# Splitting the last gather of a recurrent step into two column halves, with separate PSUM tiles for the turned halves and new issue orders

## The chip, the cores and the metric

The kernel runs on one core of a Trainium2 chip. A core has a matrix engine (TensorE, "PE" in the profile, with its weight loads as "PEld"), a vector engine (DVE), a scalar engine (ACT), a general engine (POOL) and a queue engine that issues transfers (SP; POOL issues some too). [...] The engines run their own instruction streams in order and wait for each other through semaphores.

The metric is the device time of one execution in microseconds, as the median of several runs. Before the change it is 3058.38 us (3 runs, 3051.87 to 3061.96).

## The reference

The computation is the forward and backward pass of a sum of two branches over a layer-normed input xn of 2048 rows and 512 columns: a dense branch (squared ReLU), and an attention branch that runs over 64 segments of 32 rows and hands 8 memory rows from one segment to the next. The attention branch, forward:

```python
for s in range(n_seg):                       # 64 segments of 32 rows
    h = concat([mem, x[segment s]])          # 8 memory rows + 32 rows
    q, k, v = h @ Wq, h @ Wk, h @ Wv         # 32 heads of 128
    p = softmax(mask(q k^T * scale))
    o = (p v) @ Wo                           # sum over the 32 heads
    mem = o[:8]                              # goes into the next segment
    outs.append(o[8:])
```

The result is `x + attention(xn) + dense(xn)`, and the kernel returns it with the gradients of the input, of the first memory, of the four attention weights and of the dense weights and biases for a given output gradient. Both directions of the attention are recurrent: forward, a segment's memory rows come out of the sum over heads of the segment before; backward, the gradient of a segment's memory rows comes out of three such sums (over Wq, Wk and Wv) of the segment after it.

## The kernel before

The kernel has five stages, one after the other: the dense branch with the layer norm; the forward chain of 64 steps; a stage that takes the backward pass of the memory rows ("left" rows) as far as it does not depend on the chain, with the dense weight gradients; the backward chain of 64 steps; and the attention's weight gradients. The change touches the two chains.

A step has 32 rows, so the kernel stacks four groups of eight heads into the 128 partitions. A matmul has weights of 32 columns and stands at one of four column positions of the array (`tile_position=(0, 32 * g)`), and four of them run beside each other. Work on heads is done in two halves of four heads per group, written 0 and 1 below.

In the **forward chain** (function `fwd`, lines 806 to 907) a step s computes, by the names used in the issue order: `k0mm q0mm k1mm q1mm v0mm v1mm` (projections, line 392), `..ev` (eviction from PSUM), `..fl` and `..Te` (a turn by matmul, line 165, and its eviction), `s0 s1` (scores, lines 432 and 437), `mx sb ex su rc pm` (softmax pieces on DVE and ACT), `tu` (turn of the probabilities, line 450), `w0 w1` (probabilities times values, line 547, into two pairs of PSUM banks with the tags pp0 and pp1), `oa ob` (their evictions), and `g0 g1` (the **gather**, line 460: the 32 heads times Wo, summed over the eight heads of each group into one PSUM bank R of 128 x 512). Then the end of the step: `ra rb` copy the two column halves of R into a float32 tile R4 in SBUF, one on ACT and one on DVE; `ta tb` turn R4 by four float32 matmuls with an identity (line 469) into one PSUM bank T; `HT` sums T over the four head groups for the 8 memory rows (line 482) and writes them into the next step's input X; `xt` does the same for the 24 other rows, later.

In the **backward chain** (function `bwd`, lines 1218 to 1356) a step has `o0mm o1mm` (projection of the gradient with turned Wo), `o0fl o0te` and so on, `vp0 vp1` (gradient of the values, lines 1290 and 1292), `s0 s1`, `d1 d2 d3 d4` for either half (the softmax's gradient on DVE, lines 496 to 506), `kp0 kp1 qp0 qp1` (line 547, into pp0 and pp1), evictions `kea keb qea qeb kla klb vea veb vla vlb`, six gathers `vg0 vg1 kg0 kg1 qg0 qg1` that add up in one bank R, and the same end `ra rb ta tb HT xt`. Its rows for kp and qp (`b_qN`, `b_kN`, `b_P`) come by transfers that POOL issues (`ldq ldn ldp`), others by SP (`ldk` for `b_kLs`, `vtr` for `b_vl`); POOL also makes two copies, `vc` and `pb` (lines 1252, 1253 and 1239).

Names with `L.` belong to the left rows, once in a block of four steps: in the forward chain `L.S0 L.S1 L.W0 L.W1 L.G0 L.G1 L.P0..P5 L.BT` on the matrix engine, in the backward chain `L.G0..3 L.H0..3 L.I0..3`, each eight matmuls, with `L.ra0..3` on DVE or ACT.

What runs in which order is written out by hand. `F_ORDER` and `B_ORDER` hold four lists of names, one for each step of a block; `play` (line 581) goes through them and calls each name's function, where each trailing `-` or `+` moves the name one step back or ahead (one block, with `L.`). All engines take their instructions in that order, each its own. `ENGS` says which evictions go to ACT and which to DVE. PSUM is allocated from pools as tiles: four single banks (tag "r", function `big`) that serve projections, turns, scores, R, T and left rows in turn, and the two pairs pp0 and pp1. A new tile in a bank waits until the last use of the tile before it, and instructions of two engines on one bank are kept apart.

Steps are called kind 0 to 3 below, by s mod 4 in order of issue.

## Time and profile before

| what | value |
|---|---|
| median of 3 runs | 3058.38 us (3051.87 to 3061.96) |
| profiled execution: span from first to last instruction | 3059.8 us, 109712 instructions |
| PE busy in the span | 2705.4 us (88%), 48600 matmuls |
| DVE / ACT / POOL busy | 1319.5 / 994.7 / 658.0 us |
| dense stage, up to about 297 us | 297 us, PE busy 259.4 |
| forward chain, 297 to 1179 us | 882 us, PE busy 813.4 |
| left rows backward, 1179 to 1470 us | 291 us, PE busy 216.3 |
| backward chain, 1470 to 2415 us | 945 us, PE busy 852.6 |
| weight gradients, 2415 to 3060 us | 645 us, PE busy 563.7 |
| mean granted clock of the matrix engine | 0.971 |

The profile shows one execution. A row of a timeline has its start and its length in microseconds, the engine, the source line, the operation, the tiles (output, then inputs after the arrow), the shape and a count; in brackets stands how long the engine had been idle and which engine's instruction released it. A row that merges several instructions runs from the first one's start to the last one's end. Matmuls are pipelined: one of 512 columns shows 0.38 us, but the next starts before it ends, so busy time of PE is more than the time that it streams.

### The profile page before, as it was taken

How to read it: one execution, taken by the hardware profiler on the slowest of the kernel's cores; microseconds unless marked ns; L12 is line 12 of the kernel's file. 1: busy time of each engine (PE TensorE's matmuls, PEld its weight loads, DVE VectorE, ACT ScalarE, POOL GpSimd, SP SyncE). 2: the span in 40 equal slices, each digit the busy share in tenths (PEclk: the TensorE clock that was granted, in tenths of full speed). 3: DMA queues.
4: the chain of work that ended last, by engine and by line, in shares of the span. 5: the costliest groups of instructions: out<-in, count | busy, mean ns of one | idle time of the engine just before them, and what ended most of it. 6: DMA issues, size and time to landing. Idle time of an engine off the chain costs nothing. (4 is left out here: it accounts for less than half of the span.)

```text
span 3059.8 us, 109712 instructions
## 1 busy us (share of the span) xinstructions
PE 2705.4 (88%) x48600; PEld 1386.8 (45%) x48600; DVE 1319.5 (43%) x3581; ACT 994.7 (33%) x2306; POOL 658.0 (22%) x1264
## 2 busy tenths in 40 slices
PE   8997899999999886877799899998989559999998
PEld 4453444444444444446444444444444224444443
DVE  5452566666666664334345444544545201100010
ACT  2422444444444444323333333333333101111111
POOL 0000000000000000113343433434343213322222
PEclk9998999999999998999999999999999879999999
DMA  9548375766767767777577676776777899898991
GB/s 257 185 146 250 101 188 161 189 181 172 190 168 182 165 157 192 229 230 220 149 173 174 190 187 164 177 203 169 176 200 175 238 192 217 194 211 207 204 207 39
DMA packets 794559, 566.78 MB, mean 185 GB/s; under 512 B 579409, under 2 KB 681570, under 8 KB 790754
## 3 DMA queue, kind: packets, MB, share of 16 engines
q1 hardware_dynamic: 748322, 430.47, 58.8%
q0 software_dynamic: 40528, 126.53, 13.5%
q8 instruction: 381, 6.24, 0.9%
q10 hardware_dynamic: 5232, 2.75, 0.4%
q14 instruction: 96, 0.79, 0.1%
HBM read 193.61 MB, written 238.56 MB: 141 GB/s over the span
## 5 line engine op out<-in xcount | busy, mean ns | idle before, releaser
L1505 PE MATMUL ps_gw<-gn,HNc 128*128 128x512 bf16 x1920 | 416.4, 379 | 0.0
L1505 PEld LDWEIGHTS <-HNc 128*128 128x128 bf16 x1920 | 187.8, 98 | 223.9
L374 ACT CAST f_N<-ps_proj 128x512 bf16<-128x512 f32 x320 | 185.9, 581 | 243.9 <-PE ps_proj L392 223.4
L1476 ACT CAST wt<-ps_gw 128x512 bf16<-128x512 f32 x128 | 74.4, 586 | 503.5 <-PE ps_gw L1505 474.4
L392 PEld LDWEIGHTS <-X 128*32 128x32 bf16 x6144 | 153.3, 97 | 161.3 <-DVE X L482 13.9
L835 POOL COPY kM<-f_kT 128x256 bf16<-128x256 bf16 x64 | 25.6, 401 | 786.7 <-DVE f_kT L377 594.9
L1459 DVE TENSOR_TENSOR gx<-ps_rows,gb 128x512 f32<-128x512 f32 x16 | 11.1, 692 | 420.5 <-PE ps_rows L1457 418.2
L1505 PE MATMUL ps_gw<-GOc,gn 128*128 128x512 bf16 x640 | 142.2, 385 | 54.8 <-DMA GOc<-S_GM 54.8
L460 PE MATMUL ps_gR<-Wk,gk 128*32 128x512 bf16 x2048 | 146.7, 386 | 19.4 <-ACT gk L374 12.9
L392 PE MATMUL ps_proj<-Wk,X 128*32 128x512 bf16 x2048 | 135.4, 384 | 12.6 <-DVE X L482 6.9
L460 PE MATMUL ps_gR<-Wq,gq 128*32 128x512 bf16 x2048 | 141.6, 382 | 1.2 <-issue 1.2
L374 ACT CAST gk<-b_pp 128x256 bf16<-128x256 f32 x192 | 68.8, 377 | 208.3 <-PE b_pp L547 146.6
L1477 POOL DMA_DIRECT2D out_dram<-wt x128 | 69.2, 541 | 309.5 <-ACT wt L1476 309.4
L1239 POOL COPY PD<-b_P 32x320 bf16<-32x320 bf16 x256 | 114.9, 449 | 95.3 <-PE b_pp L1292 64.4
L460 PE MATMUL ps_gR<-Wv,gv 128*32 128x512 bf16 x2048 | 133.4, 379 | 0.3 <-issue 0.3
L392 PE MATMUL ps_proj<-Wo,GT 128*32 128x512 bf16 x2048 | 123.9, 384 | 7.9 <-POOL GT L1203 6.7
L392 PE MATMUL ps_proj<-Wq,X 128*32 128x512 bf16 x2048 | 128.7, 382 | 0.0
L460 PE MATMUL ps_R<-Wo,OT 128*32 128x512 bf16 x2048 | 126.4, 388 | 0.0
L469 PE MATMUL ps_sum<-identF,R 128*128 128x128 f32 x512 | 102.4, 295 | 24.6 <-ACT R L374 18.4
L392 PE MATMUL ps_proj<-Wv,X 128*32 128x512 bf16 x2048 | 124.1, 378 | 0.0
L1505 PEld LDWEIGHTS <-gn 128*128 128x128 bf16 x640 | 63.4, 99 | 132.3 <-issue 59.6
L374 ACT CAST gON<-ps_proj 128x512 bf16<-128x512 f32 x128 | 74.9, 585 | 143.2 <-PE ps_proj L392 141.5
(260 smaller groups left out, 5128.0 us busy)
## 6 DMA issues: line engine op xcount, KB each, us to landing
S_A<-f_N SPq DMA_DIRECT2D x64, 512.0 KB
out_dram<-wt POOLq DMA_DIRECT2D x142, 128.0 KB, 4.6
S_A<-f_N SPq DMA_DIRECT2D x64, 256.0 KB
S_GB<-gv SPq DMA_DIRECT2D x32, 512.0 KB
S_GB<-gq SPq DMA_DIRECT2D x32, 512.0 KB
S_GB<-gk SPq DMA_DIRECT2D x32, 512.0 KB
b_kN<-S_A POOLq DMA_DIRECT2D x63, 256.0 KB, 5.0
b_qN<-S_A POOLq DMA_DIRECT2D x63, 256.0 KB, 5.4
```

Source lines behind the costliest of these rows:

```text
L374: nc.scalar.copy(out, in_)
L392: nc.tensor.matmul(o, lhsT=hT[:, dc, :], rhs=x, start=(dc == 0), stop=(dc == DC - 1), tile_position=(0, 32 * g))
L460: nc.tensor.matmul(o, lhsT=XT(k, g), rhs=x, start=(first and k == 4 * h), stop=(last and k == 4 * h + 3), tile_position=(0, 32 * g))
L469: nc.tensor.transpose(st["T"][:, c * P:(c + 1) * P], R4()[:, c * P:(c + 1) * P], identF[:])
L835: o["km"] = lambda: nc.gpsimd.tensor_copy(B_["kM"][:, :, :, lc], T["kT"][:, :, :, 0:M])
L1239: nc.gpsimd.tensor_copy(PD[32 * g:32 * g + 32, g], C["P"][32 * g:32 * g + 32, :, 0:L])
L1459: nc.vector.tensor_tensor(out=gx[:], in0=ps[:], in1=gb[:], op=ALU.add)
L1476: nc.scalar.copy(wt[:], ps[:])
L1477: pdma(dst, wt[:])
L1505: nc.tensor.matmul(ps[:], lhsT=l(rc), rhs=r(rc), start=(n == 0), stop=(n == RC_ALL - 1))
```

## The change

The end of a step is taken apart into two column halves, 0 to 255 and 256 to 511, in both chains.

Forward, `g0` and `g1` are done as two halves each: the left columns of all 16 head matmuls into R, then the right columns into R2, a second bank. A step issues 64 gather matmuls of 256 columns where it issued 32 of 512. `ra` and `rb` copy R and R2, and both are on ACT now. Backward, the first five gathers stay as they are; the sixth adds its left columns into R and puts its right columns alone into R2. A backward step issues 16 more gather matmuls. `ra` copies all 512 columns of R (ACT), and `rb` adds R2 onto the right half of R4 (DVE). In both, `ta` turns the left half of R4 into a tile in pp0 and `tb` the right half into one in pp1; T no longer takes one of the four single banks, and R2 does. `HT` becomes `Ha` and `Hb`, `xt` becomes `xa` and `xb`, one for each half.

Both issue orders are new throughout. In the lists, every name of a step has three or four more `+`, which shifts all by the same number of steps; beyond that, names have moved within the lists. Two moves that matter below: in the forward chain `v0mm` stands between `s0` and `s1` in three of four kinds (before in kind 0 alone), and `L.G0`, `L.G1` stand between the scores and `w0` of kind 2; in the backward chain `s1` stands ahead of `kp0` in all kinds (before in kinds 0 and 3).

```diff
-    def gather(R, XT, W, h, first, last):
+    def gather(R, XT, W, h, first, last, cs=slice(0, 4)):
         for k in range(4 * h, 4 * h + 4):
             for g in range(HG):
-                x, o = W(g * KH + k), R[32 * g:32 * g + 32, :]
-                if len(x.shape) == 3:
-                    o = o.rearrange("p (a b) -> p a b", b=P)
-                nc.tensor.matmul(o, lhsT=XT(k, g), rhs=x,
+                x = W(g * KH + k)
+                if len(x.shape) == 2:
+                    x = x.rearrange("p (a b) -> p a b", b=P)
+                nc.tensor.matmul(R[32 * g:32 * g + 32, 0:(cs.stop - cs.start) * P].rearrange("p (a b) -> p a b", b=P),
+                                 lhsT=XT(k, g), rhs=x[:, cs, :],
                                  start=(first and k == 4 * h), stop=(last and k == 4 * h + 3),
                                  tile_position=(0, 32 * g))
+    C01, C23 = slice(0, 2), slice(2, 4)
+    def in_halves(ps, alloc, XT, W, h, first, last):
+        for n, cs in (("R", C01), ("R2", C23)):
+            if n not in ps:
+                ps[n] = alloc("ps_" + n)
+            gather(ps[n], XT, W, h, first, last, cs)
+    def sum_ops(o, ps, st, R4, pair, added):
...
+        def ra():
+            n = D if added else 2 * P
+            ENGS["ra"](dst()[:, 0:n], ps["R"][:, 0:n])
+        def rb():
+            if added:
+                nc.vector.tensor_tensor(out=st["R4"][:, 2 * P:4 * P], in0=ps["R2"][:, 0:2 * P],
+                                        in1=st["R4"][:, 2 * P:4 * P], op=ALU.add)
+            else:
+                ENGS["rb"](dst()[:, 2 * P:4 * P], ps["R2"][:, 0:2 * P])
+        def tT(h):
+            st["T", h] = pair(h)
+            for c in (0, 1):
+                nc.tensor.transpose(st["T", h][:, 0, c * P:(c + 1) * P], st["R4"][:, (2 * h + c) * P:(2 * h + c + 1) * P],
+                                    identF[:])
...
+    def half_over_groups(out, T, rows):
+            nc.vector.tensor_reduce(out, T[:, 0, 0:2 * P].rearrange("p (c g r) -> p c r g", c=2, g=HG)[:, :, rows],
+                                    axis=AX.X, op=ALU.add)
...
     # forward chain, kind 2
-        "k1mm q0mm k0mm L.E3 L.E2 kl L.sx- xt- q0ev k1ev q1mm k0ev k0fl q0fl q1ev k0Te L.hl++ k1fl q0Te L.u3 k1Te "
-        "q1fl s0 mx0 q1Te s1 sb0 mx1 sb1 ex0 L.ldL+ ex1 su0 rc0 pm0 tu0 v0mm su1 v0ev rc1 pm1 v1mm L.X1 w0 v1ev "
-        "tu1 oa0 ld L.G1 w1 soV- ob0 L.t2 km ob1 oa1 L.mtr g0 g1 ra L.P5 soP rb L.E5 tb ta HT",
...
+        "L.E3+ k1mm+++ q0mm+++ km++ L.E2+ k1ev+++ soP++ L.sx q0ev+++ xb++ k0mm+++ q1mm+++ k0ev+++ k0fl+++ kl+++ "
+        "q0fl+++ xa++ q1ev+++ k0Te+++ k1fl+++ q1fl+++ q0Te+++ s0+++ L.ldL++ k1Te+++ mx0+++ q1Te+++ sb0+++ v0mm+++ "
+        "L.lo+ s1+++ L.G0+ ex0+++ su0+++ mx1+++ sb1+++ rc0+++ ex1+++ pm0+++ v0ev+++ tu0+++ v1mm+++ soN++ su1+++ "
+        "L.G1+ w0+++ rc1+++ pm1+++ ld+++ L.P5+ tu1+++ v1ev+++ oa0+++ w1+++ ob0+++ ob1+++ g0+++ oa1+++ g1+++ ra+++ "
+        "ta+++ Ha+++ rb+++ tb+++ Hb+++ ..."
...
     # backward chain, kind 2
-        "L.G3 o0mm ldn- ldk- L.ra2 o0ev kla1- o1mm o1ev ldp o0fl pb- xt- klb1- vp0 o0te s0 vea L.gs d10 vp1 vla "
-        "d20 ldq- o1fl d30 d40 vlb vg0 kp0 veb tu0 o1te keb0 qp0 s1 qea0 klb0 vg1 kea0 kla0 pb d11 d21 kg0 L.sl- "
-        "d31 vc d41 tu1 qeb0 kp1 qp1 keb1 qg0 qea1 L.gl+ kea1 kg1 qeb1 qg1 rb ra tb ta L.H3 kla1 HT",
...
+        "o0mm++++ ldq+++ xb+++ o1mm++++ o0ev++++ o0fl++++ vc+++ xa+++ o1ev++++ pb+++ o0te++++ vp0++++ s0++++ "
+        "d10++++ vea++++ d20++++ o1fl++++ vp1++++ o1te++++ vg0++++ vla++++ ldn+++ s1++++ d30++++ d40++++ d11++++ "
+        "veb++++ tu0++++ d21++++ vlb++++ kp0++++ keb0++++ vg1++++ d31++++ L.sl d41++++ qp0++++ tu1++++ L.vst+ "
+        "L.gs+ kea0++++ qea0++++ klb0++++ kla0++++ L.I3+ kg0++++ qeb0++++ kp1++++ qp1++++ qea1++++ kea1++++ "
+        "keb1++++ qeb1++++ qg0++++ klb1++++ kla1++++ L.gl++ kg1++++ qg1++++ ra++++ L.H3+ ta++++ rb++++ Ha++++ "
+        "tb++++ ldp+++++ Hb++++",
...
     # backward chain, a step's gathers
                         ps["n"] += 1
-                        gather(ps["R"], lambda k, g: G4[n][:, g, k, j, :], turned_heads(Wqkv[t]), p, ps["n"] == 1,
-                               ps["n"] == 6)
+                        if ps["n"] == 6:
+                            gather(ps["R"], x, W, p, False, True, C01)
+                            ps["R2"] = big("ps_R2")
+                            gather(ps["R2"], x, W, p, True, True, C23)
+                        else:
+                            gather(ps["R"], x, W, p, ps["n"] == 1, False)
...
+            sum_ops(o, ps, st, lambda: bt.tile([P, D], F32, name="R4", tag="R4s"),
+                    lambda h: bpp.tile([P, 2, 512], F32, name="b_T", tag="pp%d" % h), True)
```

84 lines of the change are left out of this document (47 added, 37 removed), and 50 rows, old and new, of tables (B_ORDER, F_ORDER).

## The prediction

> **What bounds the kernel now.** I read the table of stages first, then the timeline of single steps. A stage's columns are start:end, length, busy time of PE, weight loads, DVE, ACT and POOL, granted clock, DMA share, GB/s.
>
> ```profile
> 297.00:1179.00 882.00, 813.44 (x18646) 417.28 (x18650) 562.76 (x1618) 384.49 (x864) 56.91 (x153) 0.99 0.66 168
> 1470.00:2415.00 945.00, 852.63 (x21628) 436.41 (x21620) 460.21 (x1311) 339.13 (x965) 361.77 (x697) 0.99 0.70 179
> ```
>
> These are the two chains, 64 steps each: 13.8 us a forward step, 14.8 us a backward one. PE looks 90% busy, but that counts each matmul's latency (0.38 us for one of 512 columns) and the left-over work put into the chain's waits. What bounds is one step's own sequence, since step s+1 projects rows that step s computes last. The end of a forward step (second kind, s mod 4 = 1):
>
> ```profile
> 708.46 1.91 PE L460 MATMUL ps_R<-Wo,OT 128*32 128x512 bf16 x32
> ...
> 710.47 0.37 ACT L374 COPY R<-ps_R 128x256 f32<-128x256 f32 x1 [1.45 <-PE ps_R L460]
> 710.88 0.42 DVE L377 COPY R<-ps_R 128x256 f32<-128x256 f32 x1 [1.84 <-ACT R L374]
> ...
> 711.17 0.62 PE L469 MATMUL ps_sum<-identF,R 128*128 128x128 f32 x4
> 711.84 0.29 DVE L482 TENSOR_REDUCE X<-ps_sum 128x32 bf16<-128x128 f32 x1 [0.53 <-PE ps_sum L469]
> 712.18 1.05 PE L392 MATMUL ps_proj<-Wk,X 128*32 128x512 bf16 x16 [0.38 <-DVE X L482]
> ```
>
> Rows of other work are left out at the dots. From the gather's last result (708.46 + 1.91 = 710.37) to the next projection (712.18) pass 1.81 us: two copies one behind the other, transposes, one sum over the head groups.
>
> **The change part by part, forward.** In halves, R is done 8 groups of four matmuls before the gather ends. The 32 matmuls of 512 columns show 0.217 us per group of four, so each half of g1 takes 0.43. Take the gather's last result as 0. R's result stands at -0.43, ACT copies it from -0.32 to 0.05 (0.37, same lag of 0.10 as above, 710.37 to 710.47), and R2 from 0.10 to 0.48. ta starts at 0.10 and a pair of transposes needs 0.44. The sum:
>
> ```profile
> L482 DVE TENSOR_REDUCE XT<-ps_sum x64: 546/548/557, 321.3 to 1178.8; 128x96 f32<-128x384 f32 x64
> L482 DVE TENSOR_REDUCE X<-ps_sum x63: 291/292/293, 318.4 to 1160.8; 128x32 bf16<-128x128 f32 x63
> ```
>
> 128 inputs per lane take 292 ns and 384 take 548, so 1.0 ns each on 164. Ha (64 inputs) is 0.23, xa and xb (192) 0.36 each: 0.71 for 0.55, on DVE, in the projection's shadow. Ha ends at 0.81, and the projection's first eight matmuls, which in the new instruction list wait for Ha alone, start at 0.86; Hb ends at 1.24, as they end. So 0.86 instead of 1.81: **0.95 less**. The T tiles sit in pp0 and pp1, which the last evictions have left by then; only at a block's first step L.oa0 and L.ob0 stand between.
>
> The new order pays part of it back. Left work that lay in the old gap moves between scores and w0, and v0mm now goes ahead of s1. The old trace has both orders; here scores of both halves and the first w0 row of a step of kind 0 (v0mm first), then of kind 1, other rows left out:
>
> ```profile
> 689.94 0.28 PE L437 MATMUL ps_sc<-f_kT,f_qT 128*32 128x40 bf16 x16
> ...
> 691.19 0.28 PE L437 MATMUL ps_sc<-f_kT,f_qT 128*32 128x40 bf16 x16
> ...
> 693.32 0.20 PE L547 MATMUL f_pp<-ET,f_N 32*128 32x32 bf16 x4
> ```
>
> ```profile
> 703.85 0.28 PE L437 MATMUL ps_sc<-f_kT,f_qT 128*32 128x40 bf16 x16
> ...
> 704.23 0.28 PE L437 MATMUL ps_sc<-f_kT,f_qT 128*32 128x40 bf16 x16
> ...
> 706.81 0.20 PE L547 MATMUL f_pp<-ET,f_N 32*128 32x32 bf16 x4 [0.57 <-DVE ET L450]
> ```
>
> From scores to w0 pass 3.38 against 2.96, so v0mm first costs 0.42: the second half's max comes late on DVE, and su0 stands ahead of it waiting for the exponential. Kind 1 now pays that, and its gap shrinks by 0.95: 0.53 gained. Kind 2, its end before:
>
> ```profile
> 722.63 1.04 PE L460 MATMUL ps_R<-Wo,OT 128*32 128x512 bf16 x16
> ...
> 725.25 1.05 PE L460 MATMUL ps_RL<-Wo,OTL 128*32 128x512 bf16 x16
> 726.12 1.04 PE L392 MATMUL ps_proj<-Wk,X 128*32 128x512 bf16 x16
> ```
>
> The gap was 2.45 (723.67 to 726.12), because L.G0 stood last in it; it becomes 0.86, 1.59 less. L.G0, L.G1 and L.P5 go up: between scores and w0 PE now has v0mm, s1, L.G0, v1mm, L.G1, four times 0.87 and 0.4, 3.9 instead of 2.96, and w0 and L.P5 add 1.2 up to w1 where DVE's second half took 1.35: 0.8 lost, 0.75 gained in all. In kind 3 L.S0 (about 0.35, 33 matmuls) lies before ta and L.S1 after tb, as before, and DVE puts sb1 ahead of rc0, 0.14: 0.55 gained. In kind 0 L.W0 and L.BT lie before ta, and L.BT must now wait for DVE's L.E0, for R2 took the fourth bank that was free to it; DVE has L.su0 to L.E0 to do first, so its gap stays near 1.85, against 2.03: 0.2 gained. Sum 2.0 a block of four steps, times 16 blocks, 33 us. I take 27, a tenth of a us a step for lags that such a walk misses.
>
> **Backward.** One step of kind 2 before:
>
> ```profile
> 1847.33 1.91 PE L392 MATMUL ps_proj<-Wo,GT 128*32 128x512 bf16 x32
> ...
> 1850.08 0.28 PE L437 MATMUL ps_sc<-b_vT,gOT 128*32 128x40 bf16 x16
> ...
> 1851.51 0.57 DVE L506 SCALAR_TENSOR_TENSOR gS<-ds_t,b_P 128x160 bf16<-128x160 f32 x1
> ...
> 1852.70 0.37 ACT L374 CAST gk<-b_pp 128x256 bf16<-128x256 f32 x1 [1.05 <-PE b_pp L547]
> 1853.13 0.19 PE L547 MATMUL b_pp<-gST,b_kN 32*128 32x32 bf16 x2 [0.33 <-ACT gk L374]
> 1853.42 0.28 PE L437 MATMUL ps_sc<-b_vT,gOT 128*32 128x40 bf16 x16
> 1854.88 0.53 DVE L506 SCALAR_TENSOR_TENSOR gS<-ds_t,b_P 128x160 bf16<-128x160 f32 x1
> 1855.45 0.45 DVE L450 STREAM_TRANSPOSE gST<-gS 128x256 bf16<-128x256 bf16 x1
> 1855.56 0.20 PE L547 MATMUL b_pp<-gS,b_qN 32*128 32x40 bf16 x4
> ...
> 1857.64 1.05 PE L460 MATMUL ps_gR<-Wk,gk 128*32 128x512 bf16 x16 [0.34 <-DVE gk L377]
> 1858.51 1.04 PE L460 MATMUL ps_gR<-Wq,gq 128*32 128x512 bf16 x16
> ...
> 1861.37 0.61 PE L392 MATMUL ps_proj<-Wo,GT 128*32 128x512 bf16 x7
> ```
>
> 14.04 us. The second half's scores come 3.34 after the first's, because kp0 and qp0 stand ahead of them and qp0 itself waits 0.5 for ACT's copy of gk. In the new list s1 follows vg0 directly, at +4.4 instead of +6.1, and vg1 lies between kp0 and qp0, over that copy. DVE then goes from d40 (+4.8) straight into the second half: d11 to d41 at about 0.35 each and two turns of 0.45, tu1 done at +7.1 instead of +8.6. From there PE and the evictions bind: kp1 waits for ACT's last copy of half 0 (+7.85), qp1 ends at 8.5, qg0 at 9.35; kg1 starts at 9.5 when keb1 is copied, qg1's last result stands at 11.3 (before 12.2).
>
> End of the step: R at -0.43, ra now 512 wide, 0.58 by the row below, -0.32 to 0.26; then the add into R4 on DVE for 256 columns, 0.42 to take (no row; 0.42 is the same width copied, 0.68 the same operation at twice the width: these are its ends), to 0.73; tb 0.78 to 1.22, Hb to 1.49; Ha lies before it and the projection starts at 1.07. Before: 1859.55 to 1861.37, 1.82. Step: 12.4 to 12.5.
>
> ```profile
> L374 ACT CAST f_N<-ps_proj 128x512 bf16<-128x512 f32 x320 | 185.9, 581 | 243.9 <-PE ps_proj L392 223.4
> 1847.19 0.68 DVE L1173 TENSOR_TENSOR b_R<-ps_RL,b_R 128x512 f32<-128x512 f32 x1
> 1900.41 1.04 POOL L1252 COPY b_vT<-b_vl 128x1024 bf16<-128x1024 bf16 x1 [3.26 <-PE ps_sc L437]
> 1901.39 0.40 POOL L1253 COPY b_vT<-b_vTL 128x256 bf16<-128x256 bf16 x1
> 1905.65 1.96 POOL L1239 COPY PD<-b_P 32x320 bf16<-32x320 bf16 x4
> PE b_pp L1290 <- POOL PD L1239: 10.0, 11, 1.4
> b_kN<-S_A POOLq DMA_DIRECT2D x63, 256.0 KB, 5.0
> ```
>
> The same walk for the other kinds: PE has 10.3 us of its own work in a step (projection 1.73, six gathers 5.2, the rest 3.4 by its rows' spacing) and 0.43 for each L.G, L.H, L.I, stands still about 0.8 at the projection's end and in the last gap, and waits 0.3 to 0.4 for the evictions before its last two gathers. That gives 12.9 for kind 0 (four fillers), 12.7 for kind 1 (three; its PD copies, which held vp0 up to 1.4 us, now run a step earlier on POOL) and 13.35 for kind 3 (three, and L.ta and L.tb at 0.27), where L.H0 still stands ahead of the projection. Mean 12.86; I add 0.35 for lags and the stalls that the mean of 14.77 (945 / 64) holds: 13.2, and 64 x 1.55 = 99 us less.
>
> **Other costs.** [...] Elsewhere nothing changes. Sum: -27 - 99 + 3 = -123, from the profiled execution's 3059.8 to 2937; the median of the runs lies 1.4 below that span: **2936 us**.
>
> [...] The rows of 40 columns above show 0.006 us between starts (0.28 less 0.19, over 15). [...]
>
> **The rivals.**
> 1. Halved matmuls cost as much as whole ones (54 ns, not 27): 32 x 0.027 a forward step, 16 a backward step, 83 us: 3019. For it: nothing here shows 256 columns on 32-wide tiles. Against: 40-column ones are far below 54. [...]
> 2. Loads come late in part of the backward steps. kN may be loaded only when qp1 has read it (+8.1), then lands 5.0 us after issue, and on POOL vc (1.04 + 0.40) and pb (1.96) stand before that issue in two of four steps; qp0 of the next step wants it at 12.5 + 6.1. Window 10.4 from 8.2, needed 5.0 + 3.4 and an issue, 8.9. On SP, kLs queues behind a transpose that waits for vc, with about no slack in kinds 2 and 3. At 0.8 us a step lost: 2990.
> 3. The same loop becomes the bound: shorter steps load DMA more (share 0.70 now), and if landing goes from 5.0 to above 6.5 it sets the pace; 1.9 more, from 8.4 on, it eats the gain of 123. At 9.4, every step held, 2.9 x 64 = 186: 3122, slower than before. For it: the late kLs; against: 16 engines have 0.3 left.
> 4. The gain of the ends comes back as waits in the moved fillers: 3058, no change. For it: forward kind 2; against: backward fillers lie where DVE works.
>
> **How the numbers follow.** Forecast 0.64, rival 1 0.06, rival 2 0.15, rival 3 0.11, rival 4 0.04. Faster holds forecast and rivals 1 and 2: 0.85; same 0.04; slower 0.11. No change means within 0.3%, 9 us. The forecast's own range is 2890 (the walks without added lags, 33 + 114, and a little more) to 2985 (twice the lags); up to 3030 it takes in rivals 1 and 2, leaving rivals 3 and 4 and a tail below out.
>
> **What would show it.** Forward: last ps_R2 result to the first projection about 0.9 in kinds 1 and 2, 1.8 in kind 0; scores to w0 3.4. Backward: the two scores under 2 us apart, steps near 13, stage near 845 us. Wrong if PE waits for kN or kLs before qp0, if 256-column groups of four start over 0.12 apart, or if the projection waits for Hb at its first matmul.

## The result, and the profile after

The changed kernel takes 3016.98 us (median of 4 runs, 3015.03 to 3033.83) beside 3058.96 us for the kernel before on the same chip: a ratio of 0.9878, with an interval of 0.9849 to 0.9907, or 42 us less. I had forecast 2936 us, 122 less. The direction holds. The time lies above the forecast's own range (2890 to 2985) and inside the wider one, up to 3030, that was there to take in rivals 1 and 2; the gain is a third of the one forecast.

The profiled execution takes 3013.3 us, 46.5 less than the one before. Stages, from the first to the last projection of each chain in the two traces (the first matmuls of `ps_proj` with X and with GT):

```
us                                              before    after   forecast
dense branch, up to the forward chain            300.5    300.6     same
forward chain                                    868.3    846.4     -27
between the chains                               289.0    302.3     same
backward chain                                   937.8    900.3     -99
backward chain's end and weight gradients        664.2    663.7     same
```

So the forward chain did what the walk said (-21.9), the stage between the chains lost 13.3, and the backward chain gave 37.5 instead of 99. The two chains of the changed kernel in the table of stages (start:end, length, busy time of PE, weight loads, DVE, ACT, POOL, granted clock with 1 as full speed, DMA share, GB/s), and then the stretch between the chains, first before and then after:

```profile
297.00:1157.00 860.00, 804.54 (x20619) 466.01 (x20663) 533.33 (x1675) 406.86 (x928) 57.43 (x155) 0.99 0.67 172
1461.00:2362.00 901.00, 846.04 (x22612) 462.96 (x22608) 459.16 (x1435) 355.21 (x969) 357.56 (x692) 0.99 0.71 185
1168.80:1457.80 289.00, 214.74 (x4176) 142.29 (x4169) 107.33 (x240) 98.89 (x186) 61.95 (x113) 0.92 0.75 221
1146.90:1449.20 302.30, 218.05 (x4190) 147.37 (x4196) 107.25 (x240) 99.75 (x188) 62.11 (x113) 0.89 0.74 213
```

The end of a forward step of the second kind after the change, from its timeline (it answers to 708.46 to 712.18 of before):

```profile
697.19 1.93 PE L460 MATMUL ps_R<-Wo,OT 128*32 128x256 bf16 x64
...
698.79 0.76 ACT L374 COPY R<-ps_R 128x256 f32<-128x256 f32 x2 [1.02 <-PE ps_R L460]
699.21 0.82 PE L495 MATMUL f_T<-identF,R 128*128 128x128 f32 x4
...
699.69 0.23 DVE L504 TENSOR_REDUCE X<-f_T 128x16 bf16<-128x64 f32 x1 [1.91 <-PE f_T L495]
...
699.97 1.05 PE L392 MATMUL ps_proj<-Wk,X 128*32 128x512 bf16 x16
```

64 matmuls of 256 columns take 1.93 us where 32 of 512 took 1.91. The gather's last result is there at 699.12, the projection starts at 699.97: 0.85 after it, where 0.86 was forecast and 1.81 stood before. The first ACT copy starts 0.33 ahead of the gather's end.

A backward step of kind 2 after the change, the same that the prediction showed before it:

```profile
1878.43 0.28 PE L460 MATMUL ps_R<-Wq,gq 128*32 128x256 bf16 x2
...
1879.07 0.83 PE L495 MATMUL b_T<-identF,R 128*128 128x128 f32 x4
1879.83 1.91 PE L392 MATMUL ps_proj<-Wo,GT 128*32 128x512 bf16 x32
...
1882.59 0.28 PE L437 MATMUL ps_sc<-b_vT,gOT 128*32 128x40 bf16 x16
...
1884.39 0.27 PE L437 MATMUL ps_sc<-b_vT,gOT 128*32 128x40 bf16 x16
...
1889.20 0.19 PE L590 MATMUL b_pp<-gST,b_kLs 8*128 8x32 bf16 x4 [0.73 <-issue]
...
1893.38 1.48 PE L392 MATMUL ps_proj<-Wo,GT 128*32 128x512 bf16 x24
```

The second scores come 1.80 us after the first (3.34 before), the projection 1.12 after the gather's last result (1878.71 to 1879.83; 1.07 forecast). The step takes 13.55 us, and 0.9 of that passes ahead of the row at 1889.20, between two matmuls of one group with nothing that the profile shows to wait for.

Step lengths by kind, from first projection matmul to first projection matmul:

```
                 forward, median (mean)                       backward, median (mean)
         kind 0       kind 1       kind 2       kind 3        kind 0       kind 1       kind 2       kind 3
before   13.91 14.25  13.22 13.24  13.86 13.85  13.26 13.30   14.87 15.19  14.49 14.42  14.04 14.05  15.02 15.86
after    13.21 13.77  12.70 12.89  13.29 13.33  12.86 13.30   15.55 15.84  13.06 13.10  12.81 12.88  14.79 15.31
forecast        (gains 0.2, 0.53, 0.75, 0.55)                 13.25        13.05        12.80        13.70
```

The last line has the walk with its 0.35 of lags. Kinds 1 and 2 of the backward chain are where it put them; kinds 0 and 3 are 2.6 and 1.6 us longer on the mean, and 16 times the two is 67 us, a little more than the 62 that are missing. Some of PE's waits in the backward chain, us in total, times, longest, first before the change and then after it:

```profile
PE b_pp L547 <- issue: 11.6, 5, 2.7
PE b_pp L547 <- DVE gS L506: 2.6, 16, 0.2
PE ps_gR L460 <- issue: 2.5, 6, 0.6
PE b_pp L547 <- DMA b_qN<-S_A: 0.3, 1, 0.3
```

```profile
PE b_pp L590 <- issue: 15.9, 15, 2.4
PE b_pp L590 <- DVE gS L549: 8.2, 12, 1.0
PE ps_gR L460 <- issue: 5.2, 8, 1.1
PE b_pp L590 <- DMA b_kLs<-S_NL: 3.6, 4, 1.7
PE b_pp L590 <- DMA b_qN<-S_A: 3.0, 3, 1.9
```

Three things have grown: rows that come late, waits for DVE's product gS (longest 1.0 us instead of 0.2), and "issue".

**What "issue" is here.** I numbered all of PE's instructions (weight loads, matmuls and the few hundred that wait for semaphores) in the order of their starts, took each pause of over 0.45 us that began within the backward chain, and set it beside the packets of q8, the queue that carries instructions. 29 of the 71 pauses after the change begin at one and the same number modulo 256, and no other number has more than two. Six of the 29:

```
resumes at   pause   its number   number mod 256   us since the last packet of q8 had ended
1742.2       1.07    66922        106              1.41
1794.6       1.19    69482        106              1.30
1801.4       1.24    69738        106              1.59
1806.8       1.91    69994        106              1.34
1865.4       0.60    73066        106              1.39
2257.3       2.60    92778        106              1.48
```

```profile
q8 instruction: 405, 6.64, 0.9%
...
1742.24 0.83 PE L460 MATMUL ps_gR<-Wv,gv 128*32 128x512 bf16 x12 [0.68 <-issue]
...
1806.82 0.19 PE L590 MATMUL b_pp<-gST,b_kN 32*128 32x32 bf16 x3 [1.74 <-issue]
```

405 packets of 16 KB carry PE's 51,672 matmuls, as many weight loads and 385 other instructions, 256 to a packet, which I call a page (this trace lacks 138 of the matmul records, none of them within the backward chain, so the number is shifted but stays the same). The 29 pauses fall into the middle of gathers, of left rows, of kp and of qp, whatever the data, but always at the same place of a page; PE goes on 1.2 to 1.6 us after a packet has ended, and counted in order that is in all 29 the packet of that very page. I take it that PE had no code left to run; the trace shows the pause and the packet, not the cause. The late packets are no slower than the others (1.0 us, the median of both), they start later: 2.6 us after the page before has begun, by the median, and 1.2 us for the other pages. In the changed kernel the 29 waits take 32.6 us of the backward chain, 18.3 in kind 0 and 12.5 in kind 3; before, 12 took 18.3.

### The profile page after: what moved, and what is told of

Its sections match the earlier page's. It is cut to its first block, busy times and chain, and to the rows that moved or that the text cites. A ratio compares the mean times of both kernels' runs of the same rounds, so it can differ in the third digit from the quotient of the medians.

```text
span 3013.3 us, 116085 instructions
## 1 busy us (share of the span) xinstructions
PE 2695.5 (89%) x51534; PEld 1469.6 (49%) x51672; DVE 1292.7 (43%) x3772; ACT 1033.1 (34%) x2370; POOL 658.1 (22%) x1264
## 4 chain that ended last, share of the span: by engine, by line
PE 77%; DMA 9%; DVE 5%; issue 3%; SPq 3%; ACT 2%; POOL 0%; ACTq 0%; DVEq 0%; POOLq 0%
PE ps_gw L1563 18%; PE ps_proj L392 14%; PE ps_gR L460 11%; PE ps_R L460 4%; PE ps_L L350 3%; PE b_pp L590 3%; PE ps_tr L165 3%; PE ps_RL L1220 2%; PE ps_w L1088 2%; PE ps_sc L437 2%; PE ps_w L1082 2%; DMA b_kLs<-S_NL 2%; PE f_pp L590 1%; PE f_T L495 1%; PE b_T L495 1%
## 5 line engine op out<-in xcount | busy, mean ns | idle before, releaser
L1517 DVE TENSOR_TENSOR gx<-ps_rows,gb 128x512 f32<-128x512 f32 x16 | 11.1, 692 | 424.1 <-PE ps_rows L1515 424.1
L392 PE MATMUL ps_proj<-Wq,X 128*32 128x512 bf16 x2048 | 136.3, 383 | 6.8 <-DVE X L955 4.3
L460 PE MATMUL ps_gR<-Wk,gk 128*32 128x512 bf16 (+1 forms) x2048 | 133.3, 372 | 1.2 <-issue 0.7
L460 PE MATMUL ps_R<-Wo,OT 128*32 128x256 bf16 x4096 | 128.4, 280 | 1.1 <-DVE OT L377 1.1
L460 PE MATMUL ps_gR<-Wq,gq 128*32 128x512 bf16 (+1 forms) x2048 | 118.8, 341 | 3.9 <-issue 3.8
L1288 POOL DMA_DIRECT2D b_P<-S_A x63 | 33.9, 538 | 347.2 <-issue 110.4
```

What stands on the lines that cost most here:

```text
L392: nc.tensor.matmul(o, lhsT=hT[:, dc, :], rhs=x, start=(dc == 0), stop=(dc == DC - 1), tile_position=(0, 32 * g))
L460: nc.tensor.matmul(R[32 * g:32 * g + 32, 0:(cs.stop - cs.start) * P].rearrange("p (a b) -> p a b", b=P), lhsT=XT(k, g), rhs=x[:, cs, :], s ...
```

## Experiments

The runs below are from chips on which the kernel before takes 3057 to 3073 us; each is compared with it on the same chip. Chain lengths are those of the stage table, kinds are means of the backward chain, "pages" is the time that PE stood still at ends of pages in the backward chain, and "at 0.5" the time in that chain in which the granted clock of the matrix engine was 0.5. The theories below do not have the clock in them; what it does to their reading comes behind the stores.

```
run                      ratio to before [95%]      forward between backward  kind 0  kind 1  kind 2  kind 3  pages  at 0.5
(before)                 1                           868.3   289.0   937.8    15.19   14.42   14.05   15.86   18.3    19.1
(changed)                0.9878 [0.9849, 0.9907]     846.4   302.3   900.3    15.84   13.10   12.88   15.31   32.6    18.2
e9_changed_again         0.9858 [0.9826, 0.9890]     845.3   296.7   909.2    16.47   13.10   13.09   15.02   39.1    23.7
e1_forward_alone         0.9968 [0.9950, 0.9986]     846.4   298.0   945.6    15.20   14.74   14.09   15.98   19.5    32.8
e2_backward_alone        0.9894 [0.9872, 0.9915]     870.6   285.7   917.1    17.02   13.10   12.98   15.06   36.7    37.2
e3_turns_earlier         0.9837 [0.9810, 0.9863]     840.1   294.9   910.5    16.58   13.06   12.94   15.19   31.4    38.4
e4_no_chain_stores       0.9722 [0.9691, 0.9753]     846.3   297.7   870.9    14.05   13.11   12.96   15.16   17.4    16.2
e5_copy_after_loads      0.9857 [0.9824, 0.9890]     843.8   301.6   918.5    16.66   13.08   12.96   15.58   30.0    58.9
e6_two_transfers_later   0.9910 [0.9878, 0.9941]     852.3   296.5   916.0    16.35   13.20   13.02   15.55   52.1    34.0
e7_and_kLs_earlier       0.9926 [0.9899, 0.9954]     849.7   296.9   922.3    16.35   13.09   12.97   16.15   54.5    46.9
e8_three_moves           0.9883 [0.9854, 0.9912]     846.8   293.0   918.2    16.07   13.16   12.88   16.20   51.8    40.4
e10_whole_gathers        0.9938 [0.9916, 0.9960]     856.6   295.6   935.3    16.45   13.49   13.40   16.03   41.3    44.4
e11_turns_and_copy       0.9855 [0.9827, 0.9883]     847.7   293.7   907.7    16.70   13.09   12.95   14.82   31.1    40.8
e12_no_stores_and_copy   0.9709 [0.9679, 0.9740]     849.0   297.0   871.0    14.61   13.10   12.90   14.64   21.1    23.5
e13_stores_whole         0.9960 [0.9944, 0.9976]     844.4   299.1   935.2    17.95   13.16   12.97   15.21   25.4    68.3
e14_whole_turns_copy     0.9933 [0.9913, 0.9953]     847.5   289.3   925.5    17.72   13.08   12.95   14.93   15.5    71.4
```

My theory at this point: the walks were right as far as PE, DVE, ACT and POOL go, and the missing time is in transfers that crowd the stretch between two blocks (second half of kind 3, first 9 us of kind 0), and in the end of the forward chain. The rival: the new orders themselves are longer than walked.

### One chain alone

The forward chain's parts of the diff on the kernel before:

```diff
 (before.py) + in_halves, sum_ops, half_over_groups, forward order and engines; backward chain as before
```

> The changed forward chain with the backward chain of before. Theory: the two chains are independent and each keeps its share of the difference between the two traces: the forward chain (first to last projection of X) goes from 868 to about 846 us, the stage behind it gives back 7 us where the turns of the weights no longer stand in the wait for the last left softmax, and up to 6 more; so -9 to -15 us, about 3047. Rival: the 13 us that the stage behind the chain lost come from something else than the forward chain (chance, or the backward chain); then -22, about 3037, and that stage takes 289 us again.

The backward chain's parts alone:

```diff
 (before.py) + in_halves, sum_ops, half_over_groups, backward order and engines; forward chain as before
```

> The changed backward chain with the forward chain of before. Theory: -37 us, about 3021, with the same long steps of kinds 0 and 3 (15.8 and 15.3 us on the mean) and short ones of kinds 1 and 2 (13.1 and 12.9), and the stage between the chains at 289 us. Rival: the long steps come from a state that the forward chain leaves behind (DMA backlog, clock); then kinds 0 and 3 come near the 13.25 and 13.7 that I predicted and the time is near 2960.

0.9968 and 0.9894, together 0.9862 where the whole change has 0.9878 and, run again, 0.9858: the two add up. With the forward chain changed alone the stage between the chains is at 298.0 us, with the backward chain changed alone at 285.7; its loss belongs to the forward chain. The long steps of kind 0 are there without the changed forward chain (17.02). Both rivals are out.

### The stage between the chains

At the end of the forward chain the kernel turns weights for the backward pass; which ones, and where, hangs on names of the order in its last block (`after`, a dictionary of names and numbers of turns). Ten hang on `L.tu1`. Before the change that name stands ahead of `L.W0`, after it behind. Timeline of PE before, then after:

```profile
1179.14 1.70 PE L165 MATMUL ps_wt<-ident,Wk 128*128 128x128 bf16 x24
...
1186.44 0.20 PE L547 MATMUL f_pp<-ETL,vM 32*128 32x32 bf16 x4
```

```profile
1162.09 0.18 PE L590 MATMUL f_pp<-ETL,vM 32*128 32x32 bf16 x1 [3.93 <-DVE sm_rs L573]
1163.65 0.20 PE L590 MATMUL f_pp<-ETL,vM 32*128 32x32 bf16 x1 [1.38 <-DMA vM<-S_A]
...
1166.20 6.65 PE L165 MATMUL ps_wt<-ident,Wk 128*128 128x128 bf16 x80
```

Before, PE turned weights while DVE and ACT did the last left softmax. After, it waits 3.93 us for that softmax, 2.3 for the rows vM, and turns the weights afterwards. From the last X projection to the stage's first projection pass 39.5 us instead of 32.5.

```diff
-            after = {"ob0": 2, "ob1": 2, "L.tu1": 10, "L.ob1": 2, "L.G1": 1, "L.G0": 1}
+            after = {"ob0": 2, "ob1": 2, "L.tu0": 10, "L.ob1": 2, "L.G1": 1, "L.G0": 1}
```

> The changed kernel, with the ten turns of weights at the end of the forward chain hung on L.tu0, which stands ahead of L.W0, instead of L.tu1, which in the new order stands behind it. Theory: PE does these turns (6.65 us) while it waits for the left softmax (3.93 us) and for vM (2.3 us), as before the change; 4 to 6 us less than the changed kernel, about 3011. Rival: the turns' evictions get in the way of the softmax on DVE and ACT, which take their instructions in the same order, or the first projections of the next stage wait for its loads anyhow; then no change, 3017.

The wait for the softmax is gone from PE's timeline (the turns fill it, 1153.30 to 1159.35), and 0.59 of the waits for vM is left:

```profile
1159.35 0.19 PE L590 MATMUL f_pp<-ETL,vM 32*128 32x32 bf16 x3
1160.13 0.18 PE L590 MATMUL f_pp<-ETL,vM 32*128 32x32 bf16 x1 [0.59 <-DMA vM<-S_A]
```

The way to the stage's first projection takes 37.6 us, 35.7 and 34.3 to 34.5 in the three later runs with the same edit, 38.4 to 41.6 in those without it. So the mechanism is shown, with 2 to 5 us. The kernel's own time does not tell: 0.9837 beside 0.9878 and 0.9858 for the changed kernel, with intervals that overlap, and 0.9855 for e11, which has the edit too. The other 6.3 of the stage's 13.3 us are lost behind its first projection, and they go with the clock of that execution: the stage's granted clock is 0.92 before and 0.89 after (lines in the first section), by the time at 0.5 an estimated 7 us in that part. In the other kernels with the changed forward chain and without the edit the stage takes 295.6 to 301.6.

### The stretch between two blocks

Once in a block the kernel writes the gathered gradients of four steps to memory; the next block's first evictions write into the same tiles. The transfers of gk in the list of DMA issues, with count and size of one (gv and gq have the same):

```profile
S_GB<-gk SPq DMA_DIRECT2D x32, 512.0 KB
```

Six of 512 KB a block make 3 MB (the expectation below says 1.5). Without them:

```diff
+                        if b in (0, NB - 1):
                             dma(S_GB[b, t][:, gs, ks], ...)
...
-                    got[i] = rows_of(i, g, lambda b: S_GB[b, t], ...)
+                    got[i] = rows_of(i, g, lambda b: S_GB[b if b == 0 else NB - 1, t], ...)
```

> The changed kernel without the stores of the gathered gradients (S_GB, 1.5 MB a block) in all blocks but the first and the last; the weight gradients then read the first-written block again instead of theirs, as many bytes as before, so these outputs are left out in effect. Theory: the long steps of kinds 0 and 3 come from the transfers of those steps (16 DMA engines over 0.9 busy from the second half of kind 3 to 9 us into kind 0): late rows, and late pages of PE's own instructions. Then kinds 0 and 3 fall to about 13.5 and 14.2 us, PE's waits at page ends (32 us in the backward chain) go to under 10, and the time is 2970 to 2980. Rival: the new order itself makes these steps long; then the steps stay within 0.3 us and the time is 3010 to 3017.

The first 9 us of the same step of kind 0 (the thirteenth of the chain), first in the changed kernel, then without the stores:

```profile
1621.75:1630.75 9.00, 7.91 (x216) 4.55 (x212) 4.73 (x18) 4.27 (x12) 0.54 (x1) 1.00 1.16 338
```

```profile
1611.62:1620.62 9.00, 8.96 (x264) 4.96 (x260) 5.27 (x19) 4.48 (x12) 0.54 (x1) 1.00 0.33 107
```

The share of the DMA engines falls from full to 0.33, and PE issues 264 matmuls in the same time instead of 216. Kind 0 falls to 14.05 on the mean; half of its steps take 13.15 to 13.4 us, the walk's 12.9 and a little. Waits at page ends halve to 17.4 us, not to under 10. Kind 3 stays at 15.16: there I was wrong, the stores do not explain it. The chain takes 870.9 us, 29 to 38 less than the changed kernel's, where the forecast's 99 less would be 838.8; of the 32 us between, 17.4 are page ends and 9.5 waits for gS.

### Kind 3: a copy on POOL

The undisturbed step of kind 3 has 14.23 us, and ahead of kp0 PE starts nothing for 1.03 (0.66 of it idle). The rows of DVE and POOL at that wait, changed kernel:

```profile
1611.60 1.04 POOL L1306 COPY b_vT<-b_vl 128x1024 bf16<-128x1024 bf16 x1 [4.05 <-PE ps_sc L437]
1611.61 0.32 DVE L546 TENSOR_TENSOR ds_t<-ps_sc,ds_r 128x160 f32<-128x160 f32 x1
1611.96 0.85 DVE L549 SCALAR_TENSOR_TENSOR gS<-ds_t,b_P 128x160 bf16<-128x160 f32 x1
...
1612.96 0.20 PE L590 MATMUL b_pp<-gS,b_qN 32*128 32x40 bf16 x4 [0.66 <-DVE gS L549]
```

The product gS takes 0.33 us elsewhere; in all 15 steps of kind 3 it starts while POOL copies, in 11 of them it takes 0.85, and here it ends 0.17 us after the copy. The trace of before has the same on a smaller scale: gS there ends 0.17 to 0.18 us after the POOL copy that ran when it started, so it takes 0.42 in kind 3 and the 0.57 and 0.53 of the two rows of kind 2 that the prediction shows. Its neighbour on DVE, which reads one input from PSUM, is not touched (0.32), and neither are the 25 other such products of the chain that lie within a POOL copy (0.31 to 0.33). With `s1` ahead, both scores have read b_vT early, so POOL's copy for the next step now falls on the first half's product.

```diff
-        "pb+++ vp0++++ vc++++ o1fl++++ ... L.lq++ L.ldv++ qeb1++++ ..."
+        "pb+++ vp0++++ o1fl++++ ... L.lq++ L.ldv++ vc++++ qeb1++++ ..."
```

> The changed kernel, in the backward chain's kind 3 alone: POOL's copy of b_vl into b_vT (vc, 1.04 us) for the next step moved behind the block's loads of PGD and gOL on POOL. Theory: in the changed kernel DVE's product gS of the first half takes 0.85 us in that step instead of 0.33 because it runs beside that copy and ends with it, so kp0 stands still for 1.03 us; with the copy away gS takes 0.33, kp0 starts 0.5 us earlier and 16 steps give 8 us; loads of PGD come 1.5 us earlier. About 3009 beside 3017. Rival: kp0 is held by the order (the scores' place behind the second turn), and gS is long for another reason; then gS stays at 0.85 and nothing changes.

```profile
1554.58 0.33 DVE L549 SCALAR_TENSOR_TENSOR gS<-ds_t,b_P 128x160 bf16<-128x160 f32 x1
1555.05 0.20 PE L590 MATMUL b_pp<-gS,b_qN 32*128 32x40 bf16 x4
```

The rows are of the eighth step of the chain. The product is back at 0.33 in all steps of kind 3 and kp0 starts 4.9 us into the step instead of 5.44, as the theory said, and the kernel is no faster (0.9857). The wait for gS is gone from the list of PE's waits; that for b_kLs has gone from 3.6 to 9.3 us, and the time at a clock of 0.5 from 18.2 to 58.9. The runs show the product at 0.85 beside the copy and at 0.33 without it; why it is longer beside the copy they do not show.

Copy and stores both away:

> The changed kernel without the stores of the gathered gradients in all blocks but the first and last (the weight gradients read the first-written block again, so these outputs are left out in effect), and with POOL's copy behind the loads in kind 3. Theory: what my walk missed in kinds 0 and 3 is this traffic (late rows, late pages of instructions) and this copy; kind 0 has a median of 13.5 and kind 3 one of 13.8 us, near the 13.25 and 13.7 predicted with the lags, and the chain takes 855 to 865 us. Rival: with both gone another wait holds kind 3 (the scores' place behind the second turn, late b_kLs) and it stays above 14.3.

Its edit is the sum of the two. Kind 0 has a median of 13.35, and the undisturbed steps of kind 3 take 13.69 to 13.84 (five of fifteen), where 13.7 was forecast. The median of kind 3 is 14.37 and not 13.8, and the chain 871.0, as long as with the stores alone away: pages still cost 21.1 us, 10.1 of them in kind 3, where that step's own loads of the next block remain, and three steps of kind 0 take 18.7 to 19.2. So the undisturbed steps of all four kinds are where the walk put them (13.15, 13.06, 12.75 to 12.8, 13.7). That all the rest is disturbance by transfers is not shown.

### Moving the transfers

Two transfers of 256 KB out of the stretch:

```diff
 (list 0)  -L.qst at its begin          "... L.sx+ L.qst L.lq+ qeb1++++ ..."
 (list 3)  -L.lq++ ahead of L.ldv++
```

> The changed kernel, with two transfers of SP moved out of the stretch from the second half of kind 3 to 9 us into kind 0, behind the block's store of b_XT in kind 0: the store of the left gradients (L.qst, 256 KB) and the load of the next block's b_gqL (L.lq, 256 KB), which is read first in kind 1. Theory: the stores of the gathered gradients then start 2 to 3 us earlier, evictions into the same tiles no longer wait for them, and 0.5 MB of some 4 MB in that stretch is gone; kind 0 falls from 15.8 to about 14.8, 16 us less than the changed kernel, 3001. Rival: what holds kind 0 is the rate of the 16 engines over the whole stretch or PE's own pages, and half a megabyte later changes it by under 4 us; or the moved transfers make kind 1 (13.1) as much longer.

And the loads of b_kLs ahead of the stores of gk:

```diff
 (list 0, with the above)  -"L.ko0+ s1++++ d11++++ L.ko1+ ldk+++"  +"ldk+++ L.ko0+ s1++++ d11++++ L.ko1+"
```

> As the one with two transfers later, and in kind 0 SP issues the four loads of b_kLs ahead of the two stores of gk (L.ko0, L.ko1) instead of behind them. Theory: qp0 of kind 0 no longer waits for b_kLs (0.5 to 0.9 us in three of sixteen steps) but the evictions into gk wait as much longer for their stores; within 4 us of the kernel with two transfers later. Rival: late b_kLs is what sets kind 0, as I priced it in the prediction (0.8 us a step); then 8 us or more are gained.

Turns, copy and the two transfers together:

> The changed kernel with three of these moves together: the ten turns of weights earlier, POOL's copy behind the loads in kind 3, and the two transfers later. Theory: the gains are in different places and add up: 6 + 8 + 16 = 30 us less than the changed kernel, about 2987. Rival: the stretch of transfers takes back what shorter steps give, since the same bytes fall into less time; then under 15 us less.

All three miss. Kind 0 stays at 16.35, 16.35 and 16.07 beside 16.47 for the changed kernel run again, and PE's waits for pages go up to 52 to 55 us. Late rows were traded for late pages: the waits for b_kLs are 0.9 and 1.6 us in the first two, beside 3.6 and 4.1 in the two executions of the changed kernel. Why pages suffer more when two data transfers move I could not settle; the sum did not fall.

One transfer instead of two for each of gk and gq, with runs of 8 KB instead of 1 KB:

```diff
-                        dma(S_GB[b, t][:, gs, ks], G4[n][:, gs, ks].rearrange("p g k j r -> p g k (j r)"))
+                        if n == "v":
+                            dma(S_GB[b, t][:, gs, ks], G4[n][:, gs, ks].rearrange("p g k j r -> p g k (j r)"))
+                        elif ks == HALF[0]:
+                            dma(S_GB[b, t].rearrange("p g k c -> p (g k c)"), G4[n][:].rearrange("p g k j r -> p (g k j r)"))
```

> The changed kernel with the gathered gradients gk and gq of a block each written by one transfer (runs of 8 KB) instead of two by halves of the heads (runs of 1 KB). Theory: the engines' time goes with the number of pieces as well as with the bytes; the stores end earlier although they begin later, kind 0 falls by 0.5 to 1 us (16.5 to 15.5 or so) and the kernel by 8 to 16 us beside the changed kernel, 0.981 to 0.984 of the time before. Rival: bytes alone count, or the later start of the stores (they must wait for the last eviction of the block) holds the next block's evictions longer; then kind 0 is the same or longer, 0.986 or above.

> The same with the ten turns of weights earlier and POOL's copy behind the loads in kind 3. Theory: with the stretch of transfers shorter, the copy's 8 us and the turns' 4 come out as well: 0.977 to 0.981. Rival: as with the copy and the turns alone, the transfers take it back, and it equals the run with whole stores.

Worse, and by much: 0.9960 and 0.9933. Waits of PE and of ACT in the backward chain with whole stores:

```profile
PE b_pp L590 <- DMA b_qN<-S_A: 26.3, 14, 3.6
PE b_pp L590 <- issue: 11.6, 9, 2.1
...
ACT gk L374 <- DMA S_GB<-gk: 44.9, 12, 5.3
```

Pages wait less (25.4 us at page ends, 15.5 in the second run), rows of b_qN much more (26.3 us instead of 2.6 in the changed kernel run again), and ACT's evictions into gk wait 44.9 us for the store instead of 12.8, since the one store starts only when the block's last eviction is done. Fewer pieces did not pay for the later start; the two runs do not separate the one from the other.

**The clock behind a wait.** The stops themselves are not all that whole stores cost. PE's rows in a step of kind 0 of e13, and the stretch behind the long wait in it:

```profile
1568.01 0.20 PE L590 MATMUL b_pp<-gS,b_qN 32*128 32x40 bf16 x4 [2.25 <-DMA b_qN<-S_A]
...
1570.89 1.90 PE L460 MATMUL ps_gR<-Wv,gv 128*32 128x512 bf16 x16
...
1576.50 1.05 PE L460 MATMUL ps_gR<-Wq,gq 128*32 128x512 bf16 x16
```

```profile
1568.90:1575.70 6.80, 6.34 (x120) 2.38 (x112) 1.00 (x3) 1.78 (x6) 0.54 (x1) 0.50 0.31 86
```

PE stands still for 2.25 us. Then the granted clock is 0.50 for 6.8 us, and 16 matmuls of a gather take 1.90 us instead of 1.05. In the traces of all these kernels the stretches at 0.5 that begin within the backward chain last 3.41 or 6.83 us, and 123 of the 128 begin during, or at most 3.4 us after, a stop of PE of 0.8 us or more. By these 1.90 us instead of 1.05, nearly half of such a stretch is lost where PE has work throughout, so half of the column "at 0.5" is an estimate, from above, of what the clock costs: 9 and 12 us in the two executions of the changed kernel, 29 in e5, 17 to 23 in the three kernels with moved transfers, 34 and 36 with whole stores. Less that estimate, the chains of all kernels that have the changed backward chain with its column halves and its stores take 887 to 901 us. Most of what differs between these kernels is then the clock, and their times say little about the moves: the three with the copy behind the loads and the transfers in place (e5, e11, e14) are the lowest by it, at 887 to 890, so the copy may be worth what its theory said. That is not shown by a time.

The clock also differs from one execution to the next: over the whole span its mean is 0.956 to 0.967 in the ten runs of the changed kernel, and on one chip the run at 0.956 takes 3050 us where the one at 0.967 takes 3018.

### What the halves themselves give

```diff
-        for n, cs in (("R", C01), ("R2", C23)):
-            ...
+        if "R" not in ps:
+            ps["R"] = alloc("ps_R")
+        gather(ps["R"], XT, W, h, first, last)
+        ps["R2"] = ps["R"][:, 2 * P:4 * P]
...
 (backward: the sixth gather whole into R; ra copies 512 columns after it, rb is left out)
```

> The changed kernel with its issue orders and its two pairs for the turned halves, but without the column halves: every gather writes 512 columns into one bank, ra and rb copy its halves forward, and backward ra copies all 512 columns and rb is left out. Theory: halves are worth what they let run ahead of the gather's end, some 0.43 us at each step's end forward (the gap goes from 0.85 to 1.3 us) and 0.35 backward, less the 3,072 fewer matmuls, which cost nothing; 64 x 0.78 = 50 us more than the changed kernel, so the two chains would be near the time before or above, and PE's pages come 24 fewer. Rival: the gain of the change lies in the orders (s1 ahead, fillers moved), and halves only move the same wait to Hb; then under 20 us more.

> The changed kernel as it is, to have its stages and waits a second time and beside the next three. Both theories expect 0.988 of the time before, the forward steps at 13.2, 12.7, 13.3 and 12.9 us by their medians, and kind 0 of the backward chain between 15.8 and 17.0, as in the kernels tried so far that leave its transfers as they are.

0.9938 against 0.9858: 24 us by the two medians on one chip (3053.1 and 3029.2, with medians of the mean granted clock of 0.9625 and 0.962), half of my 50. Step by step the halves are worth 0.24, 0.41, 0.42 and 0.08 us forward (medians of 13.45, 13.11, 13.71 and 12.97 against 13.21, 12.70, 13.29 and 12.89), so the 0.43 is there where nothing else ends the step, in kinds 1 and 2. Backward kinds 1 and 2 lose 0.39 and 0.31 by the mean, kind 3 1.0 (with 3 us more at page ends in its steps, a new wait of 0.4 a step for an eviction, and 13.7 us at a clock of 0.5 where the other trace has none), and kind 0 nothing, as it would be where transfers set its length and a wait in its end gap costs nothing. The rest of the change's gain, some 18 us, lies in what this kernel keeps: the orders, the engines of ra and rb, and the pairs for the turned halves. No run separates these.

Turns and copy, without the moved transfers:

> The changed kernel with two of the moves: the ten turns of weights earlier, and POOL's copy behind the loads in kind 3; the two transfers of SP stay where the change has them. Theory: the turns give 5 to 7 us; the copy takes the wait of kp0 away (8 us) but the rows of b_kLs that kind 3 waits for next take most of it back, so 0.983 to 0.985 of the time before. Rival: both add up, below 0.981.

0.9855, the changed kernel again. No kernel that stores everything beats the changed one by more than the intervals.

## Why the prediction was off

**Right.** The forward walk: the end gap 0.85 us in kinds 1 and 2 (0.86), 1.58 in kind 0 (1.85), scores to w0 3.3 us in kinds 0 and 1 (3.4) and 4.06 in kind 2 (3.9), and gains of the medians of 0.70, 0.52, 0.57 and 0.40 that sum to 2.2 us a block (2.0 walked). That the sum agrees is in part luck: by kinds the walk had 0.2, 0.53, 0.75 and 0.55, and kind 0, which gained 0.5 more than walked, makes up for kinds 2 and 3. The backward walk in kinds 1 and 2 to 0.1 us, and in kinds 0 and 3 in the undisturbed steps once stores and copy are away. Rival 1, halved matmuls at the price of whole ones, is out:

```profile
L460 PE MATMUL ps_R<-Wo,OT 128*32 128x256 bf16 x4096 | 128.4, 280 | 1.1 <-DVE OT L377 1.1
```

4096 of them are busy for 128.4 us in all, and the 1.93 us for 64 give 0.030 each, latency of the last included. The sum has 3 us for the overhead of the added matmuls, an estimate of mine that no run shows; what they show is 1.93 us for 64 beside 1.91 for 32, 0.02 a step, 1.3 us in the 64 steps of the forward chain. The 0.19 in the prediction's 0.006 for 40 columns is one such matmul's own time, 0.18 to 0.19 us in the trace of before.

**Wrong, the step that failed:** "Mean 12.86; I add 0.35 for lags and the stalls that the mean of 14.77 holds". The 0.35 is right for lags (kinds 1 and 2), and holds nothing for transfers in kinds 0 and 3. What stood there instead is 2.6 us in each kind 0 and 1.6 in each kind 3: PE standing still at page ends (32.6 us in the profiled execution, 39.1 in the second, 18.3 before), late rows of b_kLs and b_qN and evictions behind the block's stores (without the stores the chain is 29 to 38 us shorter, pages included), and 0.5 in most steps of kind 3 for the copy on POOL, 8 us of PE's waits, though no kernel became faster without it. The clock is not what was missed: the chain has 19.1 us at 0.5 before and 18.2 after. With the stores away 32 of the 62 us are still missing, and beyond page ends and gS how they divide stays open. One of the prediction's own signs of being wrong shows it: PE waits for b_kLs (3.6 us).

The trace of before had it. I read the DMA share of the stage, 0.70, and gave the load loop 0.3 of room. But that share is a mean over a block. Taken from the packets by microseconds of the step, it is 0.89 to 1.08 from the sixth microsecond of kind 3 to its fifteenth before the change, and 0.01 to 0.08 from the fifth to the eighth of kind 1; after it, 0.91 to 1.17 in the first ten microseconds of kind 0 and again 0.01 to 0.07 in the fourth to eighth of kind 1. The same 3 MB must leave between two blocks, in a stretch that was full already. Rivals 2 and 3 named the late b_kLs and a load loop that becomes the bound, with chances of 0.15 and 0.11, but as one thing for all steps; it holds in two of four kinds, and in part for a queue that I had not in the sum, q8. The change also raises what that queue must bring, 405 packets of 16 KB instead of 381: some 322 matmuls a forward step instead of 291 (the counts of the two windows over 64), each with its weight load. In the forward chain, 8 waits at page ends take 11.1 us after the change (numbered by e3, whose trace lacks no records); in the forward chain of before I find none, and this is most of the difference between the 35 us that the medians of the steps gained (16 times 2.2) and the 21.9 of the stage.

**Wrong, the second step:** "Elsewhere nothing changes". The order also carries hooks that run once, at the chain's end; the ten turns lost their cover there, 7 us to the next stage's first projection.

Two slips in the working change nothing: R is done four groups of matmuls before the gather's end and not eight (the 0.43 is right), and the ends of the range do not follow from the lags, which by themselves give 2907 without them and 2965 with twice as many.

The sum, then: -21.9 forward, -37.5 backward, +13.3 between, nothing elsewhere: -46, from 3059.8 to 3013.3.

## What to carry to other kernels

Where a step gets shorter, look at the DMA share slice by slice within the period, not as the stage's mean, and count the bytes that must move between two fixed points of the period: in a full stretch, the transfers that were moved here only changed who waits. Count the instruction queue among the transfers: here q8 moved 405 packets of 16 KB, one for every 256 instructions of PE, and 29 of the 71 pauses of over 0.45 us fell on one instruction number modulo 256, 32.6 us in all; the list of waits has such pauses under "issue". Before a gain or a loss of a per cent is put down to an edit, compare the time at a lower granted clock: in e13 a stop of PE of 2.25 us had 6.8 us at a clock of 0.5 behind it, up to 3.4 us more by the estimate above. And where an order moves, look also for what hangs on its names once, at its ends.

## What the runs showed of the hardware

PE stands still at ends of pages, 0.5 to 2.6 us at a time in the changed kernel, and goes on 1.2 to 1.6 us after a packet of q8 has ended; in the backward chain that takes 17.4 and 21.1 us without the block's stores (e4, e12) and 32.6 and 39.1 with them (the two executions of the changed kernel). Behind about half of the stops of PE of a microsecond or more (127 of 263 in the backward chains of all traces here) the granted clock is at 0.5 within 3.4 us of PE's going on, in stretches of 3.41 or 6.83 us; in one of them 16 matmuls of 512 columns take 1.90 us instead of 1.05. Gather matmuls of 256 columns on 32-wide tiles take 0.030 us each (1.93 us for 64), those of 512 columns 0.060 (1.91 us for 32). Of the 15 products gS that start while POOL's copy runs in the changed kernel, 14 end 0.18 us after the copy (0.85 us in 11 of them, 0.32 to 0.33 in the 113 without a copy); before the change all 63 that start beside a copy end 0.17 to 0.18 us after it. The 26 products that read PSUM and lie within a copy take 0.31 to 0.33.
